# Product 2 starts 56 steps behind product 1 instead of 85: new hand-written orders for TensorE and ScalarE

## The chip, the cores and the metric

The kernel runs on 1 core of one Trainium2 chip. The metric is the device time of one execution in microseconds (us); less is better. TensorE (PE) multiplies, with its weight loads shown as PEld; ScalarE (ACT), VectorE (DVE) and GpSimd (POOL) compute; SyncE (SP) issues most DMAs.

## The reference, cut to what matters

```python
# x: (8, 4096, 192), weight: (8 heads, 7 taps), w_in: (192, 2048), w_out: (2048, 192), float32
w = softmax(weight, axis=-1)
x_pad = concatenate([zeros(B, 6, D), x], axis=1)
x_unf = x_pad[:, idx, :].reshape(B, S, K, H, group)    # 7 neighbouring tokens, 8 heads of 24 channels
x = einsum('hk,bskhg->bshg', w, x_unf).reshape(B * S, D)
h = x @ w_in                                           # product 1
g = h * cos(h)
out = g @ w_out                                        # product 2
```

So there are a causal convolution over 7 tokens with one set of taps a head, and two matrix products with h cos(h) between them, over 32,768 tokens.

## The kernel before

The tokens are cut into 64 tiles of 512 (`T`) and 32 units of 1024 (`U`); a unit is two tiles, the even one and the odd one (`second` is 0 or 1, line 481). The kernel's order is written by hand: a loop over tiles t (line 480) reads two strings, one for TensorE and one for ScalarE and VectorE, and issues what each word stands for. Each engine runs its own instructions in just that order and waits, where it must, for semaphores.

The words of the TensorE string (lines 468 to 474):

- `h0` to `h7` are product 1 of this tile (`mm1`, lines 387 to 397). Each makes 256 of the 2048 columns of h for 512 tokens, with 6 matmuls, into a buffer of two PSUM banks from `h_pool`. That pool has 3 buffers, and a new one is taken from it for each `h`, so the buffer of the third one before must be free.
- `c1`, `c2` are a half each of the convolution of a later unit (`conv_part`, lines 218 to 250): 4 matmuls each for 4 heads, of unit u + 2. It takes one buffer of `h_pool` too (`ring_banks`). So in tiles 2 to 59 nine buffers a tile are taken. Between `c1` and `c2` stands a turn (below).
- `m4` and the like are so many steps of product 2 (`mm2_step`, lines 412 to 445). A tile has 64 steps of two matmuls, each on half of TensorE's rows. They add into two PSUM banks of `o_p` and `o_q`, one buffer each, which must be copied out before the next tile's step 0. The row halves change banks after 32 steps, and must not be on one bank at a time. For that a **turn** (lines 162 to 173) puts a nop into SyncE's queue which waits for the two matmuls of step 31, and the weight load of step 32 waits for that nop.
- `p` stands where a tile's 64 steps are done, `q` where 32 are.

The words of the other string (lines 469, 475, 476): `s0` to `s7` are the cosine on ScalarE and the product h cos(h) on VectorE (`gcu`, lines 399 to 406), after which the buffer of that `h` is free; cosines have 3 buffers. `ec1`, `ec2` copy a convolution out of its buffer (line 209, ScalarE). `P` and `Q` copy the two banks of product 2 out (`evac`, lines 447 to 450), `P` on ScalarE and `Q` on VectorE. An item is issued when the TensorE word that it needs has been issued (`flush`, lines 490 to 508).

Work for SyncE and GpSimd is issued at two words. At `p` (lines 534 to 547): in even tiles the transpose of the next unit's convolved tokens by DMA (`turn_unit`, line 267), in odd tiles the doubling of a convolved unit on GpSimd (`double_unit`), then the store of an evacuated tile (`store(t - 2)`, line 453), and in odd tiles the loads of unit u + 4 (lines 75 and 69). At `q` (lines 526 to 533), in even tiles, GpSimd mends the edges of the transposed unit and casts the input of unit u + 3. SyncE's queue runs in order, turn nops included.

By the end of tile t's string, 64(t + 1) - 85 steps of product 2 are issued: product 2 of a tile starts behind `p` and `h3` of the next tile, in that tile's slot 3. The last tile's product 2 (lines 426 to 433) uses four separate sums, of which two sit in buffers of `h_pool`, and after it come two more passes of the loop (`NT + 2`), without product 1, for what is left.

Of the kernel before, what the change touches and what calls it, by code (L numbers as in the profile page):

```python
# [16 lines left out]
def kernel(  # L17
# [15 lines left out]
    NT = NTOK // T  # L33
    NB = T // 128
    U = 1024
    NU = NTOK // U
# [3 lines left out]
    NF = Dff // 128  # L40
# [50 lines left out]
    def cast_wo(q):  # L91
        nc.gpsimd.tensor_copy(out=wo[:, q * HP : (q + 1) * HP], in_=wo_f[:, q * HP : (q + 1) * HP])
# [118 lines left out]
    def ring_banks():  # L211
        h = h_pool.tile([128, 2, T], FP32, name="h")
        return [h[:, 0, :], h[:, 1, :]]
# [49 lines left out]
    def turn_unit(u, n0=0, n1=UB + 1):  # L263
        ct = ct_tiles.pop(u)
        if u not in cT:
            cT[u] = cT_pool.tile([128, UB + 1, NC, 128], BF16, name="cT")
        nc.sync.dma_start_transpose(out=cT[u][:, n0:n1].rearrange("p n c k -> p (n c) k"),
                                    in_=ct[:, n0:n1].rearrange("p n c t k -> p (n c t k)"))
        cT.pop(u - 2, None)
# [48 lines left out]
    for i, k in enumerate("DPDPDPADPDPADPAD"):  # L318
        q, rows = divmod(i, 4)
# [43 lines left out]
    def conv_rest():  # L363
        banks = o_banks()
        for c in range(2):
            for i in range(4):
                for prev in range(2):
                    conv_mm(0, c, [b[:, 4 * G * 2 * c :] for b in banks], i, slice(0, 128), NB + 1 - prev, UB + 1 - prev, prev,
                            start=c == 0 and prev == 0 and i % 2 == 0, stop=c == 1 and prev == 1 and i % 2 == 1)
        yield  # L370
        for b in range(2):
            for c in range(2):
                conv_out(0, c, [x[:, 4 * G * 2 * c :] for x in banks], NB, NB, UB, copies[1 - b], True, (b,))
        yield
# [37 lines left out]
    def mm2_step(q):  # L412
        tt, i = divmod(q, 2 * STEPS)
        half, k = divmod(i, STEPS)
        if tt >= NT:
            return
        if tt < NT - 1:
            f, si = divmod(k, 2)
            if i == 0:
                for b in range(2):  # L420
                    bank = o_pools[b].tile([128, T], FP32, name="o_ps%d" % b)
                    for j in range(2):
                        o_ps[tt, b, j] = bank[:, j * D : (j + 1) * D]
                    o_ps[tt, b] = bank[:, 0 : 2 * D]
            first, last = i == 0, i == 2 * STEPS - 1
        else:

            si, f = divmod(k, NF)
            if half == 0 and f == 0:
                for b in range(2):  # L430
                    o_ps[tt, b, si] = (o_pools[b].tile([128, T], FP32, name="o_ps%d" % b) if si else
                                       ring_banks()[0])[:, 0:D]
            first, last = half == 0 and f == 0, half == 1 and f == NF - 1
        ms = []
        for r in range(2):
            b = half ^ r
            rows = slice(64 * r, 64 * r + 64)
            s = 2 * b + si
            ms.append(nc.tensor.matmul(out=o_ps[tt, b, si], lhsT=g_tiles[tt][rows, f, s * 128 : (s + 1) * 128],  # L439
                                       rhs=wo[rows, f // 2, f % 2, :], start=first, stop=last, skip_group_check=True))  # L440
        if i == STEPS - 1:
            turns[tt] = Turn()
            turns[tt].mark(*ms)
        if i == STEPS:
            turns.pop(tt).wait(*ms)

    def evac(t, b):
        if t not in o_sb:
            o_sb[t] = opool.tile([128, NB, D], FP32, name="o_sb")
        copies[b](o_sb[t][:, 2 * b : 2 * b + 2, :].rearrange("p s d -> p (s d)"), o_ps.pop((t, b)))  # L450

    def store(t, b0=0, b1=NB, queue=nc.sync):
        queue.dma_start(out=out[t * T + b0 * 128 : t * T + b1 * 128, :].rearrange("(n p) d -> p n d", p=128),
                        in_=o_sb[t][:, b0:b1, :])

    def finish(t):
        o_sb[t] = opool.tile([128, NB, D], FP32, name="o_sb")
        for si in range(2):
            for b in range(2):
                copies[b](o_sb[t][:, 2 * b + si, :], o_ps.pop((t, b, si)))  # L460
                store(t, 2 * b + si, 2 * b + si + 1, [nc.scalar, nc.sync][b])
# [3 lines left out]

    PE_ORDER = "h0 m4 c1 m6 c2 m4 h1 m7 h2 p h3 m13 h4 m10 h5 m6 h6 m3 q h7 m11"
    ACT_ORDER = "s0 ec1 Q ec2 s1 P s2 s3 s4 s5 s6 s7"

    PE_FIRST = ["h0a h0b h1 h2 h3 r h4 h5 d1 d2 h6 h7 c1 c2",
                "p h0 m5 h1 m5 h2 m6 h3 m12 h4 m2 h5 m2 q d1 d2 m5 h6 m6 c1 c2 m3 h7 m3",
                "m5 h0 c1 m10 p c2 h1 h2 m7 h3 m2 h4 m14 h5 m5 h6 m4 q h7 m1",
                "m11 h0 m3 c1 m5 c2 m3 h1 m9 p h2 h3 m10 h4 m9 h5 m8 h6 m5 q h7 m11"]
    ACT_FIRST = ["s0a s0b s1 s2 er s3 s4 s5 ed1 ed2 s6 ec1 ec2 s7", "s0 s1 s2 s3 s4 s5 ed1 ed2 s6 ec1 ec2 s7",
                 "s0 P Q ec1 s1 ec2 s2 s3 s4 s5 s6 s7", ACT_ORDER]

    HALVES = {"": (0, NB), "a": (0, NB // 2), "b": (NB // 2, NB)}
    step = 0
    for t in range(NT + 2):  # L480
        u, second = divmod(t, TPU)
        cu, cc = (u + TPU, second) if t >= TPU else (1 + t, 1)
        conv = {"c": conv_part(cu, cc, ring_banks if t else o_banks, t < TPU) if cu < NU else iter(())}
        if t < TPU:
            conv["d"] = conv_part(cu, 0, ring_banks if t else o_banks, True)
        if t == 0:
            conv["r"] = conv_rest()
        act, done, h = (ACT_ORDER if t >= len(ACT_FIRST) else ACT_FIRST[t]).split(), set(), {}

        def flush():  # L490
            while act:
                k = act[0]
                need = {"P": "p", "Q": "p", "e": "r" if k == "er" else k[1:2] + "2"}.get(k[0], "h" + k[1:])
                if need not in done:
                    return
                act.pop(0)
                if k[0] in "PQ":
                    if 0 <= t - 2 < NT - 1:
                        evac(t - 2, "PQ".index(k[0]))
                elif k[0] == "e":  # L500
                    next(conv[k[1]], None)
                    if k == "er":
                        turn_unit(0, NB, UB)
                        load_unit(2)
                        load_edges(2)
                        cast_wo(0)
                elif k[0] == "s" and t < NT:
                    gcu(t, int(k[1]), h.pop(k[1:]), *HALVES[k[2:]])

        for k in (PE_ORDER if t >= len(PE_FIRST) else PE_FIRST[t]).split():  # L510
            if k[0] == "h" and t < NT:
                h[k[1:]] = mm1(t, int(k[1]), *HALVES[k[2:]])
            elif k[0] in conv:
                next(conv[k[0]], None)
            elif k[0] == "m":
                for q in range(step, step + int(k[1:])):
                    mm2_step(q)
                step += int(k[1:])
            elif k[0] == "p":
                assert step % (2 * STEPS) == 0  # L520
            elif k[0] == "q":
                assert step % (2 * STEPS) == STEPS
            done.add(k)
            flush()

            if k == "q":
                if second == 0 and t and u + 1 < NU:
                    mend_edges(u + 1)
                if t == 1:
                    cast_unit(3)  # L530
                    mend_edges(1)
                if second == 0 and u + 3 < NU:
                    cast_unit(u + 3)
            if k == "p":
                if second == 1 and t > 1 and cu < NU:
                    double_unit(cu)
                if second == 0 and t and u + 1 < NU:
                    turn_unit(u + 1)
                if t == 1:
                    turn_unit(1)  # L540
                if 0 <= t - 2 < NT - 1:
                    store(t - 2)
                if t == NT + 1:
                    finish(NT - 1)
            if k == ("p" if t > 1 else "q") and second == 1 and u + 4 < NU:
                load_unit(u + 4)
                load_edges(u + 4)
        if t == 0:
            double_unit(1)
            cast_wo(1)  # L550
            load_unit(3)
            load_edges(3)
            cast_unit(2)
        if t == 1:
            double_unit(2)
# [30 lines left out]
```

## Time and profile before

| | |
|---|---|
| device time, median of 3 runs | 715.14 us (713.11 to 715.79) |
| span of the profiled execution | 714.0 us, 1.1 under that median |
| mean granted TensorE clock | 0.998 |
| VectorE, h cos(h) (line 406) | 513 of 1220 ns, 606.4 us |
| ScalarE, cosine (line 402) | 513 of 1026 ns, 511.9 us |
| TensorE, product 2 (line 439) | 8128 matmuls, 434.9 us, overlapping in pairs |
| TensorE, product 1 (line 395) | 3078 matmuls, 413.7 us, overlapping in pairs |
| SyncE, issue of a transpose (line 267) | 32, median 4151 ns (3164 to 6758) |

The page names no execution time of its own for the profiled run; its span runs from the first to the last instruction. In the profile an instruction's duration includes the pipeline of its engine, so two matmuls that follow each other overlap in it; the distance from start to start is the better price. A row of the timeline that says x6 is six instructions merged, from the first start to the last end. In the lists of waits, the three numbers are the total, the count and the longest.

### The profile page before, as it was taken

How to read it: one execution, taken by the hardware profiler on the slowest of the kernel's cores; microseconds unless marked ns; L12 is line 12 of the kernel's file. 1: busy time of each engine (PE TensorE's matmuls, PEld its weight loads, DVE VectorE, ACT ScalarE, POOL GpSimd, SP SyncE). 2: the span in 40 equal slices, each digit the busy share in tenths (PEclk: the TensorE clock that was granted, in tenths of full speed). 3: DMA queues.
4: the chain of work that ended last, by engine and by line, in shares of the span. 5: the costliest groups of instructions: out<-in, count | busy, mean ns of one | idle time of the engine just before them, and what ended most of it. 6: DMA issues, size and time to landing. Idle time of an engine off the chain costs nothing.

```text
span 714.0 us, 26519 instructions
## 1 busy us (share of the span) xinstructions
PE 703.3 (99%) x11828; PEld 538.3 (75%) x11829; DVE 646.7 (91%) x601; ACT 590.4 (83%) x719; POOL 300.9 (42%) x307
## 2 busy tenths in 40 slices
PE   7899999999999999999999999999999999999997
PEld 3577777777777777777777777777777777777776
DVE  7799999999999999999999999999999999999995
ACT  7788888888888888888888888888888888888774
POOL 6553345553245533445543355534355533453200
PEclk9999999999999999999999999999999999999999
DMA  8954553545644535544546534445535565513402
GB/s 213 232 110 115 145 127 100 138 94 127 146 104 115 142 86 137 146 107 113 126 94 146 144 97 124 113 107 145 137 91 138 98 122 145 122 52 92 95 25 68
DMA packets 183713, 85.25 MB, mean 119 GB/s; under 512 B 111664, under 2 KB 183216, under 8 KB 183600
## 3 DMA queue, kind: packets, MB, share of 16 engines
q1 hardware_dynamic: 182888, 82.59, 48.3%
q8 instruction: 92, 1.51, 0.9%
q0 software_dynamic: 416, 0.79, 0.8%
q14 instruction: 21, 0.17, 0.1%
q10 hardware_dynamic: 296, 0.20, 0.1%
HBM read 31.36 MB, written 25.17 MB: 79 GB/s over the span
## 4 chain that ended last, share of the span: by engine, by line
PE 96%; DVE 1%; DMA 1%; ACT 1%; issue 0%; POOL 0%; POOLq 0%; SPq 0%
PE o_ps L439 47%; PE h L395 46%; PE h L194 3%; DMA cT<-ct 1%; DVE g L406 0%; ACT cs L402 0%; PE h L439 0%; DVE band L320 0%; POOL mask L131 0%; ACT mask L136 0%; ACT ct L343 0%; PE o_ps L194 0%; DVE diag L309 0%; DVE cT L361 0%; PE h L358 0%
## 5 line engine op out<-in xcount | busy, mean ns | idle before, releaser
L406 DVE TENSOR_TENSOR g<-h,cs 128x1024 bf16<-128x1024 f32 (+1 forms) x513 | 606.4, 1220 | 32.3 <-ACT cs L402 21.8
L402 ACT ACTIVATE cs<-h 128x1024 bf16<-128x1024 f32 (+1 forms) x513 | 511.9, 1026 | 102.2 <-PE h L395 68.2
L439 PEld LDWEIGHTS <-g 64*128 64x128 bf16 x8192 | 369.5, 94 | 91.2 <-issue 1.2
L439 PE MATMUL o_ps<-wo,g 64*128 64x192 bf16 x8128 | 434.9, 243 | 0.0
L395 PE MATMUL h<-cT,w 64*128 64x512 bf16 (+1 forms) x3078 | 413.7, 376 | 4.7 <-DVE g L406 2.5
L395 PEld LDWEIGHTS <-w 64*128 64x128 bf16 x3078 | 161.1, 94 | 72.4 <-issue 4.8
L292 POOL TENSOR_TENSOR edge_prod<-cT,tap 128x1008 f32<-128x1008 bf16 x30 | 67.2, 2239 | 347.0 <-DMA cT<-ct 347.0
L183 POOL CAST x_bf<-x_f 128x1728 bf16<-128x1728 f32 (+2 forms) x33 | 80.6, 2444 | 6.7 <-DMA x_f<-in_x_dram 6.7
L209 ACT CAST ct<-h 128x384 bf16<-128x384 f32 x120 | 51.8, 483 | 8.5 <-PE h L194 4.8
L450 DVE COPY o_sb<-o_ps 128x384 f32<-128x384 f32 x63 | 35.2, 558 | 23.6 <-PE o_ps L439 23.2
L258 POOL COPY ct<-ct 128x1536 bf16<-128x1536 bf16 (+1 forms) x31 | 45.6, 1472 | 3.4 <-ACT ct L209 3.4
L194 PE MATMUL h<-x_bf,band 64*128 64x192 bf16 (+1 forms) x472 | 41.0, 243 | 0.0
L297 POOL TENSOR_TENSOR edge_prod<-edge_prod 128x144 f32<-128x144 f32 x60 | 33.3, 554 | 4.7
L295 POOL TENSOR_TENSOR edge_prod<-edge_prod 128x432 f32<-128x432 f32 x30 | 30.3, 1009 | 2.4
L450 ACT COPY o_sb<-o_ps 128x384 f32<-128x384 f32 x63 | 29.8, 473 | 1.6 <-PE o_ps L439 1.6
L194 PEld LDWEIGHTS <-band 64*128 64x128 bf16 (+1 forms) x496 | 24.7, 94 | 2.1 <-issue 1.0
L298 POOL TENSOR_TENSOR cT<-edge_prod 128x144 bf16<-128x144 f32 x30 | 18.3, 608 | 2.4
L260 POOL COPY ct<-x_bf 128x192 bf16<-128x192 bf16 x60 | 19.2, 349 | 0.0
L108 PE MATMUL o_ps<-zero 128*128 128x512 bf16 x12 | 4.7, 554 | 1.3 <-DVE zero L103 1.3
L108 PEld LDWEIGHTS <-zero 128*128 128x128 bf16 x15 | 1.6, 121 | 3.3 <-issue 1.9
L460 DVE COPY o_sb<-h 128x192 f32<-128x192 f32 x1 | 0.4, 358 | 3.7 <-PE h L439 3.7
L460 ACT COPY o_sb<-h 128x192 f32<-128x192 f32 x1 | 0.3, 319 | 3.8 <-PE h L439 3.8
(62 smaller groups left out, 43.3 us busy)
## 6 DMA issues: line engine op xcount, KB each, us to landing
out_dram<-o_sb SPq DMA_DIRECT2D x63, 384.0 KB
x_f<-in_x_dram SPq DMA_DIRECT2D x30, 768.0 KB
x_f<-in_x_dram SPq DMA_DIRECT2D x31, 96.0 KB
x_f<-in_x_dram SPq DMA_DIRECT2D x4, 384.0 KB
wo_f<-in_moe_w_out_dram SPq DMA_DIRECT2D x4, 384.0 KB
w<-in_moe_w_in_dram POOLq DMA_DIRECT2D x2, 384.0 KB, 6.3
cT<-ct SPq DMA_TRANSPOSE x32
out_dram<-o_sb ACTq DMA_DIRECT2D x2, 96.0 KB
```

The costliest lines, as they stand in the source:

```text
L183: copy(out=bf[u][:, n0 + o : n1 + o, :].rearrange("p n (h k r) -> p (n h) k r", k=NC, r=R), in_=x_tiles[u][:, n0:n1, :].rearrange("p n (h ...
L194: return nc.tensor.matmul(out=ps[i // 2][:, 0 : (n1 - n0) * 2 * G].rearrange("p (n k i r) -> p i n k r", n=n1 - n0, k=NC, i=2)[:, i % 2], ...
L209: copy(o[:, :, 0, :], i[:, :, 0, :])
L258: nc.gpsimd.tensor_copy(out=ct[:, 0:nb, :, 1, :], in_=ct[:, 0:nb, :, 0, :])
L292: nc.gpsimd.tensor_tensor(out=edge_prod, in0=window, in1=tap.rearrange("p (a b k) -> p a b k", a=1, b=1).to_broadcast([128, NC * UB, K - 1 ...
L295: nc.gpsimd.tensor_tensor(out=edge_prod[:, :, :, 0:3], in0=edge_prod[:, :, :, 0:3], in1=edge_prod[:, :, :, 3:6], op=ALU.add)
L297: nc.gpsimd.tensor_tensor(out=edge_prod[:, :, :, 0], in0=edge_prod[:, :, :, 0], in1=edge_prod[:, :, :, j], op=ALU.add)
L395: nc.tensor.matmul(out=h[:, i, n0 * 128 : n1 * 128], lhsT=w[rows, k, j, :], rhs=c[rows, m0 + n0 : m0 + n1, k, :], start=(k == 0), stop=(k ...
L402: nc.scalar.activation(out=cs[:, :, part], in_=h[:, :, part], func=AF.Sin, bias=math.pi / 2.0, scale=1.0)
L406: nc.vector.tensor_tensor(out=g_tiles[t][:, 2 * j : 2 * j + 2, part], in0=h[:, :, part], in1=cs[:, :, part], op=ALU.mult)
L439: ms.append(nc.tensor.matmul(out=o_ps[tt, b, si], lhsT=g_tiles[tt][rows, f, s * 128 : (s + 1) * 128], rhs=wo[rows, f // 2, f % 2, :], star ...
L450: copies[b](o_sb[t][:, 2 * b : 2 * b + 2, :].rearrange("p s d -> p (s d)"), o_ps.pop((t, b)))
```

## The change

Product 2 of a tile starts in the same tile, behind `h7`, so that 56 steps are left at a tile's end instead of 85. `p` moves to between `h6` and `h7`, and `q` to between `h2` and `h3`. The two places at which SyncE's and GpSimd's work is issued get words of their own, `x` (as `p` before, behind `h2`) and `y` (as `q` before, behind `h6`; in tile 1 behind `h5`). The copies out move: `Q` now stands between the items s4 and s5, `P` between s5 and s6, and they are those of tile t - 1. The store stays at `x` and is that of t - 2. The runs of steps get other lengths, and there is one pass of the loop less. In the last tile's first half the four sums are made in turn, not two after two. All other functions are as they were.

```diff
-            si, f = divmod(k, NF)
+            si, f = divmod(k, NF) if half else divmod(k, 2)[::-1]
...
-    PE_ORDER = "h0 m4 c1 m6 c2 m4 h1 m7 h2 p h3 m13 h4 m10 h5 m6 h6 m3 q h7 m11"
-    ACT_ORDER = "s0 ec1 Q ec2 s1 P s2 s3 s4 s5 s6 s7"
+    PE_ORDER = "h0 m2 c1 m6 c2 h1 m8 h2 x m8 q h3 m8 h4 m16 h5 m8 h6 p y h7 m8"
+    ACT_ORDER = "s0 ec1 ec2 s1 s2 s3 s4 Q s5 P s6 s7"
 
     PE_FIRST = ["h0a h0b h1 h2 h3 r h4 h5 d1 d2 h6 h7 c1 c2",
-                "p h0 m5 h1 m5 h2 m6 h3 m12 h4 m2 h5 m2 q d1 d2 m5 h6 m6 c1 c2 m3 h7 m3",
-                "m5 h0 c1 m10 p c2 h1 h2 m7 h3 m2 h4 m14 h5 m5 h6 m4 q h7 m1",
-                "m11 h0 m3 c1 m5 c2 m3 h1 m9 p h2 h3 m10 h4 m9 h5 m8 h6 m5 q h7 m11"]
-    ACT_FIRST = ["s0a s0b s1 s2 er s3 s4 s5 ed1 ed2 s6 ec1 ec2 s7", "s0 s1 s2 s3 s4 s5 ed1 ed2 s6 ec1 ec2 s7",
-                 "s0 P Q ec1 s1 ec2 s2 s3 s4 s5 s6 s7", ACT_ORDER]
+                "x h0 m8 h1 m8 h2 m16 q d1 d2 h3 m8 h4 m8 c1 c2 m8 h5 y m8 h6 p h7 m8"]
+    ACT_FIRST = ["s0a s0b s1 s2 er s3 s4 s5 ed1 ed2 s6 ec1 ec2 s7", "s0 s1 s2 s3 ed1 ed2 s4 ec1 ec2 Q s5 P s6 s7"]
...
-    for t in range(NT + 2):
+    for t in range(NT + 1):
...
-                    if 0 <= t - 2 < NT - 1:
-                        evac(t - 2, "PQ".index(k[0]))
+                    if t - 1 < NT - 1:
+                        evac(t - 1, "PQ".index(k[0]))
...
-            if k == "q":
+            if k == "y":
...
-            if k == "p":
+            if k == "x":
...
-                if t == NT + 1:
-                    finish(NT - 1)
-            if k == ("p" if t > 1 else "q") and second == 1 and u + 4 < NU:
+            if k == "p" and t == NT:
+                finish(NT - 1)
+            if k == ("x" if t > 1 else "y") and second == 1 and u + 4 < NU:
```

## The prediction, made before the result was known

> **What bounds the kernel now.** I read the page's shares first, then its chain, then the waits, then one tile in the timeline of each engine, and SyncE's queue last.
>
> ```profile
> PE 703.3 (99%) x11828; PEld 538.3 (75%) x11829; DVE 646.7 (91%) x601; ACT 590.4 (83%) x719; POOL 300.9 (42%) x307
> ...
> PE 96%; DVE 1%; DMA 1%; ACT 1%; issue 0%; POOL 0%; POOLq 0%; SPq 0%
> ```
>
> The chain that ended last is TensorE for 96% of the span: from 36 us on every matmul follows the matmul before it. VectorE is only a little behind, at 91%. From the list of all waits:
>
> ```profile
> PE h L395 <- DVE g L406: 2.5, 6, 0.6
> ...
> SPq L167 <- PE o_ps L439: 200.3, 64, 4.6
> ```
>
> TensorE waits for a bank of the `h` ring for 2.5 us in the whole run. The turn nops (line 167) wait in SyncE's queue for the matmuls, not the other way round. Prices come from tile 32 (even, so it holds the transpose), TensorE first, then ScalarE, VectorE and SyncE:
>
> ```profile
> 359.03 0.83 PE L395 MATMUL h<-cT,w 64*128 64x512 bf16 x6
> 359.68 0.51 PE L439 MATMUL o_ps<-wo,g 64*128 64x192 bf16 x8
> 360.00 0.35 PE L194 MATMUL h<-x_bf,band 64*128 64x192 bf16 x4
> 360.17 0.68 PE L439 MATMUL o_ps<-wo,g 64*128 64x192 bf16 x12
> 360.67 0.35 PE L194 MATMUL h<-x_bf,band 64*128 64x192 bf16 x4
> 360.83 0.51 PE L439 MATMUL o_ps<-wo,g 64*128 64x192 bf16 x8
> 361.16 0.83 PE L395 MATMUL h<-cT,w 64*128 64x512 bf16 x6
> 361.81 0.76 PE L439 MATMUL o_ps<-wo,g 64*128 64x192 bf16 x14
> 362.38 1.48 PE L395 MATMUL h<-cT,w 64*128 64x512 bf16 x12
> ```
>
> ```profile
> 362.02 1.02 ACT L402 ACTIVATE cs<-h 128x1024 bf16<-128x1024 f32 x1
> 362.94 0.47 ACT L450 COPY o_sb<-o_ps 128x384 f32<-128x384 f32 x1
> 363.30 1.96 ACT L402 ACTIVATE cs<-h 128x1024 bf16<-128x1024 f32 x2
> ```
>
> ```profile
> 363.08 4.82 DVE L406 TENSOR_TENSOR g<-h,cs 128x1024 bf16<-128x1024 f32 x4
> ```
>
> ```profile
> 360.53 4.81 SPq L267 DMA_TRANSPOSE cT<-ct  x1
> 365.45 9.15 SPq L453 DMA_DIRECT2D out_dram<-o_sb  x2
> ```
>
> Ends of matmuls are modelled, so I take start to start. One `h` costs 0.65 us (361.16 to 361.81), n steps of product 2 cost 0.08n + 0.02 (m6 0.50, m7 0.57; a step is two matmuls), half a convolution (c1 or c2) 0.17. An `h` starts 0.86 before its cosine can (361.16 to 362.02), that is, 0.21 passes from its end. A cosine takes 1.03; the next follows 1.28 after its start when the copy P stands between (362.02 to 363.30). A product on VectorE takes 1.205 (4.82 for four) and starts 0.03 after its cosine. A matmul starts 0.07 after the product that frees its bank (a row at 32.25 us). The tile pitch is 10.79 (tile 2 starts at 35.50, tile 32 at 359.03), TensorE's own work.
>
> SyncE works in order. The transpose starts 0.53 after c1, whose turn nop stands just before it, and holds SyncE until 365.34. The store of that tile, ready since 363.4 when both copies had ended, goes only at 365.45: it stood behind the transpose. In `before` this is free, as the next turn nop (after `q`) comes 6 us later.
>
> **The change, part by part.** Product 2's work is the same, 64 steps a tile, in 8 runs instead of 9: TensorE's own pace stays at 10.77. Two things that hang on order change.
>
> *First, the ring.* The pool has 3 buffers and a tile takes 9 (h0, c, h1 ... h7), so each takes the bank of the third before it: h0 after product 5 of the last tile, c after product 6, **h1 after product 7**, h3 after the convolution's copies. In the new order the way from h1 to the end of product 7 is, counted from the start of h1:
>
> h1 0.65, m8 0.66, h2 0.65, m8 0.66, h3 0.65, m8 0.66, h4 0.65, m16 1.30, h5 0.65, m8 0.66, h6 0.65: **7.84**. Cosine 6 starts at 8.05 (0.21 later; through cosine 5 and P it would be 6.53 + 0.21 + 1.28 = 8.02) and ends at 9.08. Product 6 starts at 9.11 (product 5, behind Q, ends at about 9.10), product 7 ends at 9.11 + 2.41 = 11.52, and the next h1 starts at **11.59**. That loop is longer than TensorE's 10.77, so a tile lasts 11.6. In the old order VectorE's products 5, 6, 7 run from 368.15, so product 7 ends at 371.77, 10.6 after that tile's h1 (361.16): just below 10.79, so the wait didn't show. What grows it is m16 ahead of h5, and Q and P among the last products.
>
> *Second, the turn nop.* The nop that separates the halves of product 2 is put into SyncE's queue after step 31. In the new order that is the m8 right behind `x`, where (in even tiles) transpose and store are issued; step 32 is right behind h3. From the start of h1: c1 waits for product 6, so starts 1.20 before h1; transpose at -1.20 + 0.53 = -0.67; it takes 4.38 (mean of the 29 rows of tiles 2 to 58, 4.07 to 5.34), so ends at 3.71; store 0.11 later for 0.52, until 4.34; nop and TensorE's waking 0.10, an estimate under the 0.32 of the one wait for a nop in `before`: 4.44. TensorE stands there since the end of h3, at 3.27. **Stall 1.17** in even tiles; odd ones have a store and two loads (0.38, 0.50, 0.80) there and are done before. The two add up: h4, h5 and h6, which the loop needs, come behind the stall. The store itself is ready when SyncE reaches it (both copies ended in the tile before), so it adds its issue alone.
>
> The m8 behind h7 is the first to write the evacuated banks: Q ends at about 7.96, P at 8.2, the m8 comes at 8.49 or later. Costed at nothing with 0.3 to spare; a copy later than that would cost its lateness.
>
> A pair of tiles lasts 23.18 + 1.17 = 24.35 against 21.58. Tiles 2 to 59 have a convolution: 29 pairs, 29 x 2.77 = **+80.3**.
>
> *Start and end.* Tile 1 does 18 steps more ahead of tile 2's h0 (72, not 54): +1.44, about 0.2 of it in TensorE's 0.41 idle at 32 us: +1.2. From tile 60 on, 29 steps fewer are left: -2.3. The last tile's product 2 now takes two ring banks right after h7 (lines 431 and 432), so waits for product 6: h7 ends at 8.49, product 6 at 10.32, +1.9. With a little of a last stall in tile 60, without convolution: about -0.4 + 0.3. Together +1.1. Moved POOL work (casts, edges) stays at its places after h2 and h6 with over 5 us of slack before its next reader; costed at nothing, its price if that fails would be a wait of h0 for the edges.
>
> Sum against the profiled execution: 714.0 + 80.3 + 1.1 = 795.4 span. The median of the runs shown (715.14) is 1.1 above that span, so 796.
>
> Bounds: transposes of 4.07 throughout give -9, of 4.8 +12; 0.15 us in the loop's hand-overs are 58 x 0.15 = 9 either way. Own range 778 to 812.
>
> **Rivals.** *One wait only (0.16).* If SyncE isn't held by the transpose the turn costs nothing: 714 + 1.1 + 29 x 1.60 = 761, 762 by the median. For it: nothing in the queue; against it: the late store. The Trainium skill, page "DMA: Bandwidth & Descriptors", section "Anatomy of one DMA", puts the sequencer's dispatch of a DMA at about 50 ns (for GpSimd's path); the rows here have 4.07 us and more for a transpose on SyncE, so I go by them. If instead the ring doesn't bind (the bank of h1 free sooner than counted), c1 starts 0.83 after h0, SyncE is through at 0.83 + 0.53 + 4.38 + 0.11 + 0.52 + 0.10 = 6.47, h3 ends at 4.94: stall 1.53, 29 x 1.53 = 44: 760 again.
>
> *TensorE's pace holds (0.06), the other side.* Both loops slide under TensorE's 10.77, the way the ring does in `before`: that needs the way from h1 to product 7 shorter by 0.8 and SyncE free 1.5 sooner. Then 62 x 0.02 less for one run of steps fewer, 1.2 more at the start, 0.4 to 2.3 less at the end: 712 to 714 span, 714 by the median, not slower. Against it: ACT and DVE rows give no 0.8.
>
> *The clock falls (0.05).* In the profile TensorE stands still from 20.50 to 22.47, and is granted 0.55 and 0.50 until 26. Were each stall of an even tile to do the same, 3.4 us at half clock cost 1.7 a pair: 49 more, about 845. Against it: from 15.8 to 19.2 us TensorE is busy for 2.22 of 3.4 us at clock 1.00, no more than it would be around a stall here. The Trainium skill, page "TensorE: Matmul & The Clock Gate", section "HAM oscillation", names gaps over 3.4 us as harmful; the row shows 2.0 us enough, so the rule's margin isn't relied on, and by rule alone this rival would be nil.
>
> **Chances.** Forecast 0.73, one wait only 0.16, pace holds 0.06, clock 0.05. The range takes forecast and one wait: 757 to 812, 0.85 or a little more. About 0.5% (3.6 us) is what a measurement can tell from no change: faster 0.02 and same 0.04 (both from the pace that holds), slower 0.94.
>
> **What would show it.** Tile starts 11.6 apart (odd) and about 12.75 (even). Waits of TensorE's weight load at line 439 for line 167: some 30 times, near 1.2. Matmuls of lines 395 and 194 waiting for products of line 406 for some 0.8 a tile. In SyncE's queue transpose, store, then at once the nop, with TensorE waiting. Granted clock 1.00 after 26 us. If tile pitch is 10.8 in odd tiles the ring step is wrong; if even and odd tiles are alike the turn step is wrong.

## The result, and the profile after

The changed kernel takes 795.29 us (median of 4 runs, 794.78 to 795.70), the kernel before 715.46 beside it: ratio **1.1134, 95% interval 1.1111 to 1.1157**. The profiled execution took 795.70 with a span of 794.0, 80.0 more than the span before. The forecast was 796. (Executions of the kernel before lie near 713.3, with a mean granted clock of 0.999 or 1.000, or near 715.5, with 0.998; each experiment below is compared with those made beside it, whose median was 713.4.)

The page, busy time and the chain that ended last:

```profile
PE 728.9 (92%) x11828; PEld 526.3 (66%) x11829; DVE 652.6 (82%) x601; ACT 597.2 (75%) x719; POOL 301.6 (38%) x307
...
PE 53%; DVE 20%; SPq 11%; ACT 9%; issue 6%; DMA 1%; POOL 0%; ACTq 0%; POOLq 0%
```

No engine is full any more, though each has the same work to do. TensorE's share of the chain fell from 96% to 53%; VectorE, ScalarE and SyncE's queue, which computes nothing, stand in it now. That is what a chain through waits looks like: work that before lay beside TensorE's is now between its matmuls. The list of waits names two of them (total, count, longest):

```profile
PEld L439 <- SPq L167: 46.7, 32, 2.0
PE o_ps L439 <- SPq L167: 31.8, 29, 1.6
...
PE h L194 <- DVE g L406: 14.8, 58, 0.3
```

Product 2 waits for the turn nop in 29 tiles, and c1 waits for a product on VectorE in 58. The second looks small because matmuls' ends are modelled and rows overlap: a wait is counted only from the end of the row before it, nearly 0.2 us after the next matmul could have started. The wait of h1 is hardly in the list at all. Starts tell more. One even tile on TensorE, from the timeline (start, duration, idle before):

```profile
401.46 0.83 PE L395 MATMUL h<-cT,w 64*128 64x512 bf16 x6
402.11 0.34 PE L439 MATMUL o_ps<-wo,g 64*128 64x192 bf16 x4
402.70 0.34 PE L194 MATMUL h<-x_bf,band 64*128 64x192 bf16 x4 [0.25 <-DVE g L406]
402.88 0.66 PE L439 MATMUL o_ps<-wo,g 64*128 64x192 bf16 x12
403.38 0.33 PE L194 MATMUL h<-x_bf,band 64*128 64x192 bf16 x4
403.83 0.82 PE L395 MATMUL h<-cT,w 64*128 64x512 bf16 x6
...
406.44 0.83 PE L395 MATMUL h<-cT,w 64*128 64x512 bf16 x6
408.17 0.83 PE L439 MATMUL o_ps<-wo,g 64*128 64x192 bf16 x16 [0.89 <-SPq L167]
```

m2 needs 0.18, so c1 could start at 402.29 and starts at 402.70: 0.41 lost. h1 could start at 403.55 and starts at 403.83: 0.28, of which 0.12 lie behind the end of the row before it (403.71). In all 58 tiles with a convolution h1 starts 0.05 after product 7 of the tile before has ended. h3 is through at 407.09, step 32 starts at 408.17: 1.08. The chain, in order of time, for that stall and for the hand-over to the c1 of two tiles later (start, time, what):

```profile
403.28 4.15 SPq L267
407.42 0.05 issue
407.47 0.03 SPq L453
407.50 0.04 issue
407.54 0.51 SPq L453
408.05 0.05 issue
408.10 0.02 SPq L167
408.12 0.05 issue
408.17 0.83 PE o_ps L439 x16
...
424.57 0.95 ACT cs L402
425.52 0.02 issue
425.54 1.24 DVE g L406
426.77 0.05 issue
426.82 0.36 PE h L194 x4
```

SyncE: transpose (line 267), store (453), nop (167), and 0.05 later the matmul. The nop doesn't wait for the transposed tokens to land: GpSimd, which does, starts 1.4 to 3.6 us after the transpose lets go of SyncE's queue in these 29 tiles (at 409.39 here), the nop 0.7 after it. Then cosine 6, product 6, and 0.05 later c1.

By starts of VectorE's product 0, every odd tile lasts 11.52, every even one 12.52 to 13.26, 12.80 in the mean. Tiles 60 to 62, which have no convolution and so take eight buffers and not nine, last 10.46, just as before the change: a first sign that neither the shorter lag nor the new order of the copies is what costs.

### The profile page after: what moved, and what is told of

It is laid out like the page before. It is cut to its first block, busy times and chain, and to the rows that moved or that the text cites. A ratio compares the mean times of both kernels' runs of the same rounds, so it can differ in the third digit from the quotient of the medians.

```text
span 794.0 us, 26546 instructions
## 1 busy us (share of the span) xinstructions
PE 728.9 (92%) x11828; PEld 526.3 (66%) x11829; DVE 652.6 (82%) x601; ACT 597.2 (75%) x719; POOL 301.6 (38%) x307
## 4 chain that ended last, share of the span: by engine, by line
PE 53%; DVE 20%; SPq 11%; ACT 9%; issue 6%; DMA 1%; POOL 0%; ACTq 0%; POOLq 0%
PE o_ps L439 27%; PE h L395 24%; DVE g L406 18%; SPq L267 9%; ACT cs L402 6%; ACT o_sb L450 2%; SPq L453 2%; DVE o_sb L450 2%; PE h L194 1%; DMA cT<-ct 1%; PE h L439 0%; DVE band L320 0%; POOL mask L131 0%; SPq L167 0%; ACT mask L136 0%
## 5 line engine op out<-in xcount | busy, mean ns | idle before, releaser
L406 DVE TENSOR_TENSOR g<-h,cs 128x1024 bf16<-128x1024 f32 (+1 forms) x513 | 613.7, 1218 | 109.4 <-ACT cs L402 94.7
L402 ACT ACTIVATE cs<-h 128x1024 bf16<-128x1024 f32 (+1 forms) x513 | 517.5, 1022 | 160.2 <-PE h L395 150.2
L439 PE MATMUL o_ps<-wo,g 64*128 64x192 bf16 x8128 | 425.0, 243 | 31.8 <-SPq L167 31.8
L439 PEld LDWEIGHTS <-g 64*128 64x128 bf16 x8192 | 359.9, 94 | 137.3 <-SPq L167 46.7
L395 PEld LDWEIGHTS <-w 64*128 64x128 bf16 x3078 | 153.6, 94 | 92.9 <-issue 19.7
L194 PEld LDWEIGHTS <-band 64*128 64x128 bf16 (+1 forms) x496 | 22.2, 94 | 27.5 <-DVE g L406 13.4
L439 PE MATMUL h<-wo,g 64*128 64x192 bf16 x64 | 4.5, 243 | 1.6 <-DVE g L406 1.5
```

The source lines that it names most:

```text
L194: return nc.tensor.matmul(out=ps[i // 2][:, 0 : (n1 - n0) * 2 * G].rearrange("p (n k i r) -> p i n k r", n=n1 - n0, k=NC, i=2)[:, i % 2], ...
L395: nc.tensor.matmul(out=h[:, i, n0 * 128 : n1 * 128], lhsT=w[rows, k, j, :], rhs=c[rows, m0 + n0 : m0 + n1, k, :], start=(k == 0), stop=(k ...
L402: nc.scalar.activation(out=cs[:, :, part], in_=h[:, :, part], func=AF.Sin, bias=math.pi / 2.0, scale=1.0)
L406: nc.vector.tensor_tensor(out=g_tiles[t][:, 2 * j : 2 * j + 2, part], in0=h[:, :, part], in1=cs[:, :, part], op=ALU.mult)
```

## The experiments

My theory was the prediction's: two waits, one behind the other, for the turn nop (0.0 in odd tiles, 1.28 in even ones) and for the ring (0.73 in each: 11.52 less 10.79). **Rival A** said that product 2 now follows product 1 too closely, so its data or the evacuated banks are late. **Rival B** said that the two waits cover each other. All experiments but one, which starts from the kernel before, keep the lag of 56 steps, the order of the items for ScalarE and VectorE with `Q` and `P` in it, and all of the work, and change only the order named.

**Work issued behind `q`.** `x` moves past the last eight steps of the half, so that the nop stands ahead of the transpose.

```diff
-    PE_ORDER = "h0 m2 c1 m6 c2 h1 m8 h2 x m8 q h3 m8 h4 m16 h5 m8 h6 p y h7 m8"
+    PE_ORDER = "h0 m2 c1 m6 c2 h1 m8 h2 m8 q x h3 m8 h4 m16 h5 m8 h6 p y h7 m8"
```

> SyncE's and GpSimd's work is issued behind q instead of ahead of the last eight steps before it, so the turn nop no longer stands behind the transpose; all else as in the changed kernel. Theory (two waits in series, 1.28 us in even tiles for the turn nop, 0.73 us in every tile for the ring): even tiles fall from 12.80 to the 11.52 of odd ones, 795.3 - 29 x 1.28 - 1 = about 758. Rival A (product 2 follows product 1 too closely, its data or the evacuated banks are what is late): no change, about 795. Rival B (the two waits cover each other, so that taking one away brings out the other): even tiles stay near 12.8, about 790.

758.57 (ratio to the kernel before 1.063, 1.0608 to 1.0652), and even tiles last 11.52 like odd ones. Its timeline, TensorE and then SyncE, in an even tile:

```profile
387.00 0.83 PE L395 MATMUL h<-cT,w 64*128 64x512 bf16 x6
387.65 0.84 PE L439 MATMUL o_ps<-wo,g 64*128 64x192 bf16 x16
388.31 0.83 PE L395 MATMUL h<-cT,w 64*128 64x512 bf16 x6
```

```profile
387.41 4.84 SPq L267 DMA_TRANSPOSE cT<-ct  x1
392.36 0.51 SPq L453 DMA_DIRECT2D out_dram<-o_sb  x1
```

The transpose still holds SyncE for 4.84 us, but begins behind the nop: step 32 follows h3 after 0.65, its bare time. So the turn nop accounts for 36.7 us of the 80, and rivals A and B are out for this part.

**Steps moved ahead of h1, work issued as in the change.** The stretch from h1 to h6 falls from 48 steps to 39.

```diff
-    PE_ORDER = "h0 m2 c1 m6 c2 h1 m8 h2 x m8 q h3 m8 h4 m16 h5 m8 h6 p y h7 m8"
+    PE_ORDER = "h0 m7 c1 m5 c2 m5 h1 m6 h2 x m1 q h3 m11 h4 m5 h5 m16 p h6 y h7 m8"
```

> Lag and issue place as in the changed kernel, but steps of product 2 are moved out of the stretch from h1 to h6 (48 to 39 steps) to ahead of h1, so that the ring's loop falls to about TensorE's own pace. Theory: odd tiles 10.9 (a second loop, from h2 through products 6, 7 and 0, then binds by 0.1). In even tiles TensorE is earlier at step 32 while the transpose isn't, so the stall grows from 1.28 to about 1.8: even tiles 12.7, sum about 776. Simple addition of the two waits, which I hold for wrong here, would give 795.3 - 58 x 0.65 = 757. Rival A: no change in odd tiles, 795. Rival B (the waits cover each other): odd and even alike, about 760.

778.23 (1.0905, 1.0863 to 1.0948), the middle of two executions, 776.01 and 780.46; the second was profiled. Odd tiles last 10.80 or 10.81 (two of them 10.85 and 11.20), so the ring's wait is gone there; even ones last 12.52 to 13.3, with three of 14.7 to 14.9. The list of waits of this kernel:

```profile
PEld L439 <- SPq L167: 69.7, 35, 2.8
PE o_ps L439 <- SPq L167: 53.2, 30, 2.3
```

The stall grew, as expected (53.2 against 31.8; by starts 1.99 in the mean against 1.28): SyncE's time is fixed from c1 on, and TensorE now gets from c1 to the end of h3 0.70 sooner, by the 0.28 that h1 no longer waits and by five steps fewer on that way (17, not 22), so it only waits longer. All nine steps that were taken out of the stretch stood ahead of step 32. The way round of an even tile, from c1 over SyncE's queue to step 32, then 32 steps to h6, cosine 6, product 6 and the next c1, is as long as before: 12.78 in the mean of the 26 other even tiles, 12.80 in the changed kernel. In even tiles the two waits do cover each other in this direction, as rival B said; its 760 for the whole was wrong. Taking the ring's wait away alone therefore brought 17 us (with some 5 lost again to the three long tiles of the profiled execution), taking the nop's alone 36.7, and it matters which goes first. The long tiles are told of in the last section.

**Both edits.**

```diff
-    PE_ORDER = "h0 m2 c1 m6 c2 h1 m8 h2 x m8 q h3 m8 h4 m16 h5 m8 h6 p y h7 m8"
+    PE_ORDER = "h0 m7 c1 m5 c2 m5 h1 m6 h2 m1 q x h3 m11 h4 m5 h5 m16 p h6 y h7 m8"
```

> Both edits of the two kernels before: the lag stays 56 steps, the evacuation stays behind s4 and s5. Theory: every tile 10.9, about 724, so nine tenths of the loss is gone with the lag unchanged. Rival A (the lag itself costs): 785 to 795. Rival B: about 757, as one wait remains under the other.

717.02 against 713.47 beside it: 1.0053, 1.0034 to 1.0072. Every tile lasts 10.80 or 10.81. The page:

```profile
PE 702.4 (98%) x11829; PEld 524.1 (73%) x11829; DVE 638.1 (89%) x601; ACT 602.0 (84%) x719; POOL 300.8 (42%) x307
```

TensorE is full again. Rival A is refuted: with the same lag and the same copies, 78 us are gone, and 3.5 (0.5%) are left against the executions beside it. Of these about 1.2 lie in tiles 2 to 59, where c1 still starts 0.05 after product 6: the ring's loop now lasts 10.80 to 10.81, just above the 10.79 of the kernel before. Where the rest lies isn't shown. My own 724 was 7 too high; it had a second loop, from h2 over products 6, 7 and 0, at 10.9, and that doesn't bind.

**Work issued at the start of a tile**, ahead of c1 (GpSimd's doubling behind `q`).

```diff
-    PE_ORDER = "h0 m2 c1 m6 c2 h1 m8 h2 x m8 q h3 m8 h4 m16 h5 m8 h6 p y h7 m8"
+    PE_ORDER = "x h0 m2 c1 m6 c2 h1 m8 h2 m8 q h3 m8 h4 m16 h5 m8 h6 p y h7 m8"
...
-            if k == "x":
-                if second == 1 and t > 1 and cu < NU:
-                    double_unit(cu)
+            if k == "q" and second == 1 and t > 1 and cu < NU:
+                double_unit(cu)
+            if k == "x":
```

> SyncE's work is issued at the very start of a tile, ahead of c1, and GpSimd's doubling behind q. The transpose is then in SyncE's queue ahead of the convolution's turn nop, on which c2 waits. Theory (a nop waits for whatever stands ahead of it in SyncE's queue): the turn of product 2 is free, but c2 in even tiles waits from about 1.9 to 4.8 after h0, even tiles 14.1, odd 11.5, about 833. Rival A: no change, 795. Rival C (a nop is late only for the memory traffic of the transpose, not for the queue): 795 or less, as the transpose is then over sooner.

871.88 (1.2218, 1.2192 to 1.2243). The wait moved to the other nop, as the theory has it, and rival C is out: the transpose starts sooner (1.57 ahead of c1, not 0.57 behind it) and the kernel is slower. SyncE and TensorE in one even tile, then three stretches of 3.41 us (columns: stretch and length, busy time and count of PE, PEld, DVE, ACT and POOL, granted clock, DMA share, GB/s):

```profile
413.19 4.08 SPq L267 DMA_TRANSPOSE cT<-ct  x1
417.39 0.51 SPq L453 DMA_DIRECT2D out_dram<-o_sb  x1
```

```profile
418.03 0.34 PE L194 MATMUL h<-x_bf,band 64*128 64x192 bf16 x4 [2.43 <-SPq L167]
418.20 0.81 PE L395 MATMUL h<-cT,w 64*128 64x512 bf16 x6
418.85 1.01 PE L439 MATMUL o_ps<-wo,g 64*128 64x192 bf16 x16
419.65 1.49 PE L395 MATMUL h<-cT,w 64*128 64x512 bf16 x6
```

```profile
415.94:419.35 3.41, 1.32 (x24) 0.97 (x25) 1.03 (x1) 0.90 (x3) 0.04 (x1) 1.00 1.11 246
419.35:422.76 3.41, 3.41 (x34) 2.27 (x32) 1.75 (x2) 1.92 (x2) 3.25 (x3) 0.50 0.11 35
422.76:426.17 3.41, 3.41 (x64) 2.60 (x62) 2.40 (x3) 2.05 (x2) 3.25 (x4) 1.00 0.02 5
```

c2 waits for the nop, which waits for transpose and store. But I expected 833. The 39 us more are the clock: after the stall, TensorE is granted 0.50 for 3.41 us. That happens in 26 of the 29 even tiles; the three without it last 13.84 to 13.88 (14.1 was expected), the others 15.5 to 16.2. 26 x 1.7 = 44, less 29 x 0.2 for the stall that I set too long, gives the 39.

**Four steps more in the loop**, and **m16 at another place in it**, both on top of the kernel with work behind `q`.

```diff
-    PE_ORDER = "h0 m2 c1 m6 c2 h1 m8 h2 m8 q x h3 m8 h4 m16 h5 m8 h6 p y h7 m8"
+    PE_ORDER = "h0 c1 m4 c2 h1 m10 h2 m10 q x h3 m8 h4 m16 h5 m8 h6 p y h7 m8"
...
+    PE_ORDER = "h0 m2 c1 m6 c2 h1 m8 h2 m8 q x h3 m8 h4 m8 h5 m16 h6 p y h7 m8"
```

> The kernel that issues SyncE's work behind q (no late nop any more), with four steps of product 2 more between h1 and h6 (52, not 48) and four fewer ahead of h1. Theory (the tile is the way from h1 over cosine 6 and products 6 and 7 to the next h1): 4 x 0.08 = 0.32 longer in each of 58 tiles, 11.84 a tile, 758.6 + 18.6 = 777. Rival A (the lag or the evacuated banks): no change, 759. Rival D (VectorE's total work sets the 11.52): no change, 759.

> The same kernel with work behind q, but the run of sixteen steps stands behind h5 instead of ahead of it, and eight ahead; the sum from h1 to h6 is the same. Theory: 11.52 a tile as before it, 758.6. My prediction's words, that m16 ahead of h5 makes the loop long, would be too narrow then: only the sum counts. Rival E (it is cosine 5 and the copies behind it that are late, because h5 is): cosine 5 and P come 0.64 earlier, so 58 x 0.64 = 37 less, about 722.

778.78 (1.0914, 1.0895 to 1.0932) and 758.04 (1.0623, 1.0605 to 1.0641). Four steps more between h1 and h6 make a tile 11.85, 0.33 longer, though TensorE's work is the same: the loop it is, and not VectorE's total (rival D). (777 was expected; about 1 us of the difference lies behind the start of tile 60, where tiles last 10.72 and not 10.46.) m16 behind h5 leaves 11.52: the sum between h1 and h6 counts and not the place of m16, and cosine 5 with the copies behind it (rival E) isn't the limit.

**The start filled.** Both profiles show TensorE idle for 2.0 and 2.3 us ahead of tile 1 and then at half clock. Sixteen steps of product 2 of tile 0 go there, in the kernel before and in the one with both edits.

```diff
-                "p h0 m5 h1 m5 h2 m6 h3 m12 h4 m2 h5 m2 q d1 d2 m5 h6 m6 c1 c2 m3 h7 m3",
-                "m5 h0 c1 m10 p c2 h1 h2 m7 h3 m2 h4 m14 h5 m5 h6 m4 q h7 m1",
+                "p m16 h0 h1 h2 h3 m12 h4 m2 h5 m2 q d1 d2 m5 h6 m6 c1 c2 m3 h7 m3",
+                "m13 h0 c1 m2 p c2 h1 h2 m7 h3 m2 h4 m14 h5 m5 h6 m4 q h7 m1",
...
-                "x h0 m8 h1 m8 h2 m16 q d1 d2 h3 m8 h4 m8 c1 c2 m8 h5 y m8 h6 p h7 m8"]
+                "x m16 h0 h1 h2 m16 q d1 d2 h3 m8 h4 m8 c1 c2 m8 h5 y m8 h6 p h7 m8"]
```

> The kernel before with its orders, but sixteen steps of product 2 of tile 0 run ahead of h0 in tile 1, in the 2 us in which TensorE waits for the transposed tokens, and eight more of tile 1's steps ahead of h0 in tile 2. Theory from the profile (2.0 us of idle TensorE, then 3.4 us at half clock): up to 1.3 of work moved into the idle time and 1.7 of half clock saved, less what then waits for VectorE and the second transpose: 1.5 to 3 us less than before, 711 to 712. Rival: tile 2 starts no sooner, as the second transpose and the edges are what it waits for: no change.

> The kernel with both edits (issue behind q, steps ahead of h1), lag 56, with sixteen steps of product 2 of tile 0 run ahead of h0 in tile 1 as well. Theory: as in the kernel before, 1.5 to 3 us less than the 717.0 of that kernel: 714 to 715.5, no measurable difference from before. Rival: tile 2 waits for the second transpose anyway, no change: 717.

714.59 against 713.38 (1.0014, 1.0005 to 1.0023), and 718.28 (1.0062, 1.0049 to 1.0076). Neither gains; both expectations missed. In the first, h3 of tile 1 then waits 1.08 us for VectorE, and h2 of tile 2 1.12. In the second, TensorE waits 2.10 for GpSimd's cast and 1.25 for a turn nop behind tile 1's long transpose (7.60), so work was moved to other idle time. The first expectation also counted on 1.7 us of half clock that most executions of the kernel before don't have: one stretch of 3.41 us at 0.50 takes 0.0024 off the mean granted clock, and of the 17 beside it 14 are at 0.999 or 1.000, as are all 11 of this version. Against the profiled execution of the kernel before, which has that stretch, the filled start does gain: its span is 712.8, not 714.0. No version run here beats the median of the kernel before.

## Why the prediction was right

The measured terms come from starts of h0 in the two profiles.

| term | predicted | measured |
|---|---|---|
| odd tile, the ring's loop | 11.59 | 11.52 |
| stall of even tiles, turn nop | 1.17 | 1.28 |
| pair of tiles against 21.58 | +2.77 | +2.74 |
| 29 pairs | +80.3 | +79.6 |
| start, to h0 of tile 2 | +1.2 | +0.95 |
| from h0 of tile 60 to the end | -0.1 | -0.52 |
| sum | +81.4 | +80.0 |

**The bound.** Right: with TensorE at 96% of the chain, a wait put between its matmuls counts in full, and the two waits measured come to 79.5 of the 80.0.

**The ring.** Right in mechanism and place: c1 waits for product 6 and h1 for product 7. The loop is 0.07 shorter: products 6 and 7 take 2.35 (1.14 from start to start, the last with its full 1.21), not 2.41, and h1 starts 0.05 behind product 7, not 0.07. One sentence of the step, on what makes the loop grow, was too narrow: it is neither m16's place nor Q and P, as the run with m16 behind h5 and the same 11.52 shows, but the sum of work between h1 and h6. The old order has 36 steps of product 2 there, the new one 48, and the start of h6 came 6.21 after that of h1 and now comes 7.19 after it. The old loop so takes 10.54, which is 0.25 under the tile's 10.79; the twelve steps use that up and add 0.73.

**The turn nop.** Right, and the size too low by 0.11. The transposes took 4.35 in the mean (4.38 assumed), but they began 0.04 later behind c1, the store, the nop and TensorE's waking took 0.01 more, and TensorE was through with h3 a little sooner (4.39 after c1, not 4.47).

**The sum of the two.** Right that they add, since h4 to h6, which the loop needs, stand behind the stall: 58 x 0.73 + 29 x 1.28 = 79.5. The rival "one wait only" was priced at 760 to 762 whichever wait was gone. Without the nop's wait it came to 758.57. Without the ring's it came to 778.23, but in another order, so that run is no test of the 1.53 that the rival counted: with five steps fewer between c1 and step 32 the stall is 1.99, and it brings the clock down now and then.

**The clock.** The rival's price held (1.7 a fall), and the changed kernel has no fall after that of its start, which ends at 26.6 us. The argument against it was thinner than it looked: the stretch that it cites has 1.18 us of idle time in 3.4, and stretches of 3.41 us around a stall here have up to 1.56. The falls of the last section begin at 1.96, so the margin was some 0.4 us, which the prediction didn't know.

**Start and end.** Small, and both parts right in sign. They came out 0.25 and 0.4 below the forecast, which is about half of the 1.4 by which the sum was too high; the pairs are the other half. The wait of the last tile for two ring banks is there: 0.47 and 1.01 of idle time for line 406.

## What to carry to other kernels

A synchronization nop in a queue that also issues transfers is as late as whatever stands ahead of it: ask of each one which instruction is the next ahead of it in that queue, and how long that holds the queue (4 us and more for a transpose here, 0.4 to 0.5 for a plain store). In a hand-written order with a ring of buffers, add up each loop from taking a buffer over its consumers to taking it again; when one is longer than the busiest engine's own work, it sets the pace although no engine is full. Two such waits in a row are worth different amounts, depending on which is taken away first: here 36.7 us or 17 alone, 78 together.

## What the runs showed of the hardware

The granted clock falls to 0.50 for 3.41 us when TensorE was idle for about 2 us or more within one stretch of 3.41 us that ends there, and these stretches follow each other at fixed times. Over the profiles of the ten kernels here, cut that way (idle time from the modelled ends), the 33 falls ahead of a run's last microseconds all came behind stretches with 1.96 to 2.81 us of idle time. Three stretches with 1.98 to 2.02 had none, so by these ends the border isn't sharp, and every other stretch had less. The three long tiles of the kernel with steps ahead of h1 are such cases; two of their stretches, and one just short of it (same columns as above):

```profile
87.65:91.06 3.41, 1.30 (x24) 0.81 (x22) 3.30 (x3) 1.82 (x2) 0.00 (x0) 1.00 1.09 243
326.58:329.99 3.41, 1.27 (x26) 1.12 (x28) 2.64 (x3) 1.17 (x2) 0.04 (x1) 1.00 1.00 250
302.70:306.10 3.40, 1.40 (x28) 1.16 (x30) 2.58 (x3) 1.11 (x2) 0.56 (x1) 1.00 1.09 272
```

With 1.30 and 1.27 us of work in it the clock fell, with 1.40 it didn't. So whether a 2 us gap costs 1.7 us more depends on where it falls among these stretches: eight more single gaps of 2.05 to 2.28 us in the same kernel, each cut in two by the end of a stretch, brought no fall. The Trainium skill, page "TensorE: Matmul & The Clock Gate", section "What's actually happening", has a free-running window of 3413 ns. The stretches of 3.41 us in the traces agree with it. The Trainium skill, the same page, section "HAM oscillation", warns of gaps over 3.4 us. Here single gaps of 2.1 us sufficed (the first of the stretches shown), so the measurement decides.
